# Slot work moved up behind the masks, three scatters a period, earlier fetches, and first-layer quarters in alternating PSUM tiles: a fused linear-attention and expert-layer kernel on one NeuronCore

## The chip, the cores and the metric

The kernel runs on one core of a Trainium2 chip. The metric is the device time of one execution in microseconds (us), lower is better; three runs of the kernel before took 453.21, 453.23 and 459.25 us, median 453.23. The engines are TensorE (PE; its weight loads are PEld), VectorE (DVE), ScalarE (ACT), GpSimd (POOL) and SyncE (SP), which here issues loads. ScalarE and GpSimd issue transfers too; those with row indices (gathers and scatters) come from GpSimd.

## The reference

The first half is causal linear attention with a decay for each head, over 4 batches, 8 heads, 768 tokens and head size 64, in blocks of 64. The second half gives each of the 3072 tokens (512 features) to one of 8 experts and applies that expert's two layers.

```python
# attention, for each block of 64 positions
intra = ((qb @ kb^T) * Dmask) @ vb                 # Dmask[i,j] = lam^(i-j) for i >= j
inter = (qb * lam^(pos+1)) @ kv_state
out[block] = intra + inter
kv_state = lam^64 * kv_state + (kb * lam^(63-pos))^T @ vb
# experts
logits = x @ w_gate + modality_bias[modality_id]
e_idx  = argmax(logits);  gate_w = softmax(logits)[e_idx]
for e in range(8):
    mask = e_idx == e
    out[mask] = gate_w[mask] * (relu(x[mask] @ w1[e]) @ w2[e])     # w1: 512x1024, w2: 1024x512
```

All in float32.

## The kernel before, in words

**Attention loop (0 to about 108 us).** The 24 chunks of 128 tokens (six a batch) are worked in 12 pairs, one a *period* (`for j in range(1, pairs + 1)`). A period issues the pair's `scores` (TensorE), `masked` (VectorE), `keys` and `queries` (VectorE), `from_state`, two `outputs` (TensorE, with a ScalarE copy each), `key_values` (TensorE), and `carried` (GpSimd multiplies the old state into `faded`, L265; VectorE adds). In between it turns the pair before into token rows: `tokens` (L296, TensorE, with a ScalarE copy to `xn`, L297), which also carry the gate's products, and go to the DRAM table `xs`. `gated` (VectorE) sums the gate's products of the pair before that.

**Slots.** After a batch's last pair, `route` finds each token's expert as a one-hot `oh` (VectorE); `ranks` counts on TensorE how many tokens stand before it; `places` (VectorE) makes of this the row `sloti` of the token in a table `inv` in DRAM (an area for each expert) and the gate's weight in `pay`, with one exponential on ScalarE, and adds the batch's counts to `ohsum`. `write_slot` scatters one chunk's 128 entries to `inv` by an indirect DMA (L390, on GpSimd), so 24 in all; before the change `places` comes after the state's products, `sloti` has one buffer, and there are two scatters a period. After two batches `early_list` counts tokens per expert (`count_tiles`) and names two full tiles of 256 tokens of one expert each: **A0** and **A1**. Their expert is in `listA`; A0's weights w1 and w2 (2 MB each, four loads into `raw1`, `raw2`) are fetched in the loop, `fetch_idx` (L567, SP) reads a tile's token numbers from `inv`, and `fetch_rows` (L577, GpSimd) gathers its token rows from `xs` into `xg`.

**Expert tiles.** A float32 matmul is made of three in fp32r (`three`, L617, L620, L621): high times high, high times low, low times high. `split` makes the two parts of an operand: a ScalarE cast (L549) and a VectorE subtraction (L550). A *wide* tile turns 256 rows (`turn_rows`, TensorE transposes L610 and two splits to `xh`, `xl`), does its first layer in four quarters, **q0** to **q3**, of 24 matmuls each (`wide`), whose results ScalarE takes as `hh` (L637, relu) and VectorE as the low part `hl` (L638), with the split of a quarter of w2 behind each (`tail`); then the second layer (`second`, 96 matmuls of 512 columns) from `hh`, `hl`, `w2h`, `w2l`. PSUM has two buffers of the name `s`; before the change q0 and q1 share the first, q2 and q3 the second.

**The order of the stages.** A0's first layer; the slots of the last two batches (`write_slots`, `places`, L366 to L383), a second count and `late_list`, a chain of small VectorE operations that makes the list of all other tiles, `listB`; A1's first layer; two *thin* tiles (64 and 32 rows) with weights from the list; then ten wide tiles, the first of which I call **tile 4**; then up to seven more that run only if needed. The list's last row is written at L537. Weights of a next tile are fetched (L594, L600, L721, on SP) when the tile's regs have been read.

**What sets the order.** A scheduler places the instructions of each engine; `pinned` ties an operation behind the one pinned before it on the same engine, and `behind(a, b)` a behind b (with `wait=False`: only its place, not a wait). In `wide` of the kernel before nothing is pinned.

Of the kernel before, what the change touches and what calls it, by code (L numbers as in the profile page):

```python
# [6 lines left out]
F32 = mybir.dt.float32  # L7
# [8 lines left out]
P = 128  # L16
# [3 lines left out]
HB = 2  # L20
# [20 lines left out]
def linear_attention_moe(tc, qkv, lam, modality, wg, mbias, w1, w2, out):  # L41
    nc = tc.nc
    with ExitStack() as ctx:
# [288 lines left out]
        def ranks(b, l, mxb, m8, oh, after=None):  # L332
# [11 lines left out]
            rk = ps.tile(shape, F32, name="kv" if after is None else "x", bufs=1)  # L344
            mm = pinned(nc.tensor.matmul(rk, lowb, oh, start=True, stop=False))
            if after is not None:
                behind(mm, after, wait=False)
# [5 lines left out]
        def places(b, l, mxb, m8, oh, rk):  # L353
# [12 lines left out]
            nc.vector.tensor_tensor(out=pos, in0=oh, in1=rk, op=ALU.mult)  # L366
            slot = t2("slot")
            nc.vector.tensor_reduce(out=slot, in_=pos, axis=AX, op=ALU.add)
            sloti = t2("sloti", I32)
# [3 lines left out]
            nc.vector.tensor_tensor(out=sloti, in0=slot, in1=m8s, op=ALU.add)  # L373

            pinned(nc.vector.tensor_tensor(out=l, in0=l, in1=mxb, op=ALU.subtract))
            nc.scalar.activation(out=l, in_=l, func=AF.Exp)
            sm = t2("sm")
            nc.vector.tensor_reduce(out=sm, in_=l, axis=AX, op=ALU.add)
            nc.vector.tensor_scalar(out=sm, in0=sm, scalar1=1e-9, scalar2=None, op0=ALU.add)
            nc.vector.reciprocal(out=pay[:, cs, 1].bitcast(F32), in_=sm)  # L380
            ohn = work.tile([P, E], F32, name="ohn", bufs=1)
            pinned(nc.vector.tensor_reduce(out=ohn, in_=oh.rearrange("p c e -> p e c"), axis=AX, op=ALU.add))
            nc.vector.tensor_tensor(out=ohsum, in0=ohsum, in1=ohn, op=ALU.add)  # L383
            return [(b * NC + c, sloti[:, c : c + 1]) for c in range(NC)]
# [13 lines left out]
        def count_tiles(first, nm):  # L398

            cp = ps.tile([P, E], F32, name="o", bufs=2) if nm == "A" else ps.tile([P, E], F32, name="kv", bufs=1)  # L400
# [39 lines left out]
        def early_list():  # L440
# [4 lines left out]
            nc.vector.tensor_scalar(out=delta, in0=full, scalar1=-1.0, scalar2=float(CAP // TT), op0=ALU.mult, op1=ALU.add)  # L445
            _, ex, at = tile_list(full, delta, None, EARLY, "A", ends)
            taken = const.tile([1, EARLY], F32, name="taken")
            nc.vector.tensor_copy(out=taken, in_=ex)
            nc.vector.tensor_scalar(out=ex, in0=ex, scalar1=float(E - 1), scalar2=None, op0=ALU.min)
            nc.vector.tensor_copy(out=listA[:, 0, :], in_=ex)  # L450
            nc.vector.tensor_scalar(out=listA[:, 1, :], in0=at, scalar1=float(TT), scalar2=None, op0=ALU.mult)
            nc.vector.tensor_tensor(out=listA[:, 2, 1:], in0=ex[:, 1:], in1=ex[:, : EARLY - 1], op=ALU.not_equal)
# [3 lines left out]
            nc.vector.tensor_tensor(out=took, in0=sidx[:, :E].unsqueeze(2).to_broadcast(sh),  # L456
                                    in1=taken.unsqueeze(1).to_broadcast(sh), op=ALU.is_equal)
            nA = const.tile([1, E], F32, name="nA")
            nc.vector.tensor_reduce(out=nA, in_=took, axis=AX, op=ALU.add)
            yield ex, nA  # L460

        def late_list(exA, nA):

            cnt, n2 = count_tiles(XT + 1, "B")
# [83 lines left out]
        def split(src, hi, lo, after=None, late=False):  # L548
            cp = nc.scalar.copy(out=hi, in_=src)  # L549
            df = nc.vector.tensor_tensor(out=lo, in0=src, in1=hi.bitcast(F32), op=ALU.subtract)  # L550
            if after is not None:
                behind(cp, after)
            if late:
                behind(cp, copies[-1], wait=False)
                behind(df, logits[-1], wait=False)
            return cp, df
# [35 lines left out]
        def fetch_w1(er, kw, after=None):  # L592
            for i in range(4):
                ld = nc.sync.dma_start(out=raw1[i], in_=w1[bass.ds(er, 1), :, i].rearrange("o p k f -> p (o k) f"), **kw)  # L594
                if after is not None:
                    behind(ld, after)
# [7 lines left out]
        def turn_rows(cols, before=None, part=range(2)):  # L604
            for i in part:
# [8 lines left out]
                split(tp[:, :, :cols], xh[i][:, :, :cols], xl[i][:, :, :cols])  # L614

        def three(out, ah, al, bh, bl, first, last, before=None):
            mm = nc.tensor.matmul(out, ah, bh, start=first, stop=False)  # L617
            if before is not None:
                behind(mm, before, wait=False)
            nc.tensor.matmul(out, ah, bl, start=False, stop=False)  # L620
            return nc.tensor.matmul(out, al, bh, start=False, stop=last)  # L621

        def wide(tail, before=None):

            for i in range(4):
                if i % 2 == 0:
                    pair = ps.tile([P, 2, 2, TT], F32, name="s", bufs=2)
                hp = pair[:, i % 2]
# [6 lines left out]
                if i == 0:  # L635
                    begun = mm
                act = nc.scalar.activation(out=hh[i], in_=hp, func=AF.Relu)  # L637
                nc.vector.scalar_tensor_tensor(out=hl[i], in0=hp, scalar=0.0, in1=hh[i].bitcast(F32),  # L638
                                               op0=ALU.max, op1=ALU.subtract)
                tail(i, act)  # L640
            return begun, mm
# [64 lines left out]
        def tail(i, act):  # L706
            for op, urgent in zip(split(raw2[i], w2h[i], w2l[i]), (act, ranked[-1])):
                behind(op, urgent, wait=False)
# [68 lines left out]
        routed, slots = None, []  # L777
# [59 lines left out]
        for j in range(1, pairs + 1):  # L837
            last = j == pairs
            turns = turned(j - 1)
            gs = (HB * j, HB * j + 1)  # L840
            if not last:
                sps = [scores(g) for g in gs]
# [208 lines left out]
```

## Time and profile before

| | |
|---|---|
| runs | 453.21, 453.23, 459.25 us; median 453.23 |
| profiled execution | 452.03 us, of which the span is 450.1 us |
| busy in the span | PE 409.3 us (91%), DVE 245.3 (55%), ACT 182.6 (41%), POOL 102.7 (23%) |
| attention loop | 0 to 108 us |
| A0 | first layer 122.24 to 143.87 us, second to 154.84 |
| A1 | first layer 154.84 to 171.11 us |
| thin tiles, then tile 4's first layer | from 171 us; tile 4's second layer begins at 213 |
| the other wide tiles | 213 to the end |

The span runs from the first to the last instruction; the rest of an execution's time lies around it. A row of a timeline gives start, duration, engine, line and operation with output and inputs, and in brackets how long the engine had been idle before it and what ended that. The clock (PEclk) is the share of full speed that was granted to TensorE: 1.00 is 2.4 GHz, about 0.5 is 1.2 GHz.

### The profile page before, as it was taken

The page shows a single profiled execution, that of the slowest core. Times are in us where ns is not written, and L with a number is a line of the kernel's source. Part 1 is how long each engine was busy: PE and PEld are TensorE (multiplying, and loading weights), DVE is VectorE, ACT ScalarE, POOL GpSimd, SP SyncE. Part 2 cuts the span into 40 slices and gives each one's busy share as a digit, 9 for nine tenths or more (in the row PEclk, how much of TensorE's full clock was granted, in tenths as well). Part 3 has the DMA queues.
Part 4 walks back from the last instruction along what each step waited for, and adds up shares of the span by engine and source line. Part 5 has one row for each costly group of instructions (what it writes and reads, how often), then busy time and mean ns, then how long its engine had stood idle before and what let it go on. Part 6 is the DMA issues. An engine that isn't in the chain of part 4 may idle for free. (4 is left out here: it accounts for less than half of the span.)

```text
span 450.1 us, 9891 instructions
## 1 busy us (share of the span) xinstructions
PE 409.3 (91%) x3864; PEld 362.3 (81%) x3864; DVE 245.3 (55%) x431; ACT 182.6 (41%) x277; POOL 102.7 (23%) x116
## 2 busy tenths in 40 slices
PE   8899999996677989997999999999999999999880
PEld 4699989895476878686898989898989989998760
DVE  4677877885188551166374655646372819090510
ACT  1124232244274131256363736455454637372410
POOL 5010134251366330050202020202011111101010
PEclk9999999999596999998999999999999999999995
DMA  6999998988400023711205466501111111101000
GB/s 206 352 367 386 374 365 300 369 285 302 123 29 2 26 84 128 294 34 26 74 23 167 164 225 247 212 27 51 48 50 48 51 47 43 48 1 48 1 28 17
DMA packets 25654, 63.84 MB, mean 142 GB/s; under 512 B 7157, under 2 KB 8701, under 8 KB 25600
## 3 DMA queue, kind: packets, MB, share of 16 engines
q1 hardware_dynamic: 17360, 43.36, 27.5%
q0 software_dynamic: 4768, 13.08, 9.0%
q10 hardware_dynamic: 3472, 6.69, 3.9%
q8 instruction: 32, 0.52, 0.5%
q14 instruction: 22, 0.18, 0.1%
HBM read 91.40 MB, written 14.07 MB: 234 GB/s over the span
## 5 line engine op out<-in xcount | busy, mean ns | idle before, releaser
L617 PE MATMUL s<-xh,w1h 128*128 128x256 f32 x384 | 112.2, 292 | 10.8 <-DVE hl L638 10.2
L621 PE MATMUL s<-xh,w1l 128*128 128x256 f32 x384 | 109.8, 287 | 1.2 <-DVE w1l L550 1.2
L620 PE MATMUL s<-xl,w1h 128*128 128x256 f32 x384 | 110.0, 287 | 0.0
L550 DVE TENSOR_TENSOR w1l<-raw,w1h 128x1024 fp32r<-128x1024 f32 x48 | 58.4, 1227 | 87.9 <-ACT w1h L549 87.2
L617 PEld LDWEIGHTS s<-xh,w1h 128*128 128x128 f32 x384 | 74.7, 195 | 16.6 <-DVE hl L638 15.5
L621 PEld LDWEIGHTS s<-xh,w1l 128*128 128x128 f32 x384 | 74.6, 194 | 1.6 <-DVE w1l L550 1.6
L617 PE MATMUL o<-w2h,hh 128*128 128x512 f32 x192 | 75.7, 394 | 0.0
L620 PEld LDWEIGHTS s<-xl,w1h 128*128 128x128 f32 x384 | 74.8, 195 | 0.6 <-issue 0.2
L621 PE MATMUL o<-w2h,hl 128*128 128x512 f32 x192 | 74.8, 389 | 0.0
L620 PE MATMUL o<-w2l,hh 128*128 128x512 f32 x192 | 74.7, 389 | 0.0
L549 ACT CAST w1h<-raw 128x1024 fp32r<-128x1024 f32 x48 | 49.8, 1051 | 36.4 <-PE s L620 23.3
L550 DVE TENSOR_TENSOR w2l<-raw,w2h 128x1024 fp32r<-128x1024 f32 x48 | 58.5, 1219 | 2.0 <-ACT w2h L549 2.0
L549 ACT CAST w2h<-raw 128x1024 fp32r<-128x1024 f32 x48 | 49.9, 1039 | 0.0
L638 DVE SCALAR_TENSOR_TENSOR hl<-s,hh 128x512 fp32r<-128x512 f32 x48 | 32.9, 685 | 25.4 <-ACT hh L637 25.4
L700 ACT ACTIVATE y<-o,idx 128x512 f32<-128x512 f32 x20 | 13.8, 690 | 79.0 <-PE o L621 46.2
L701 POOL DMA_INDIRECT out_dram<-y,idx x20 | 20.2, 1008 | 111.7 <-ACT y L700 107.3
L577 POOL DMA_INDIRECT xg<-xs,idx x20 | 21.8, 1092 | 91.2 <-PE kv L610 86.3
L621 PEld LDWEIGHTS o<-w2h,hl 128*128 128x128 f32 x192 | 36.0, 188 | 7.6
L620 PEld LDWEIGHTS o<-w2l,hh 128*128 128x128 f32 x192 | 36.1, 188 | 7.1
L617 PEld LDWEIGHTS o<-w2h,hh 128*128 128x128 f32 x192 | 36.1, 188 | 7.1
L390 POOL DMA_INDIRECT inv<-pay,sloti x24 | 31.7, 1321 | 34.4 <-PE o L285 8.2
L637 ACT ACTIVATE hh<-s 128x512 fp32r<-128x512 f32 x48 | 28.5, 594 | 26.9 <-PE s L621 26.9
(213 smaller groups left out, 470.1 us busy)
## 6 DMA issues: line engine op xcount, KB each, us to landing
raw<-in_w_dram SPq DMA_DIRECT2D x104, 512.0 KB
load<-in_qkv_dram SPq DMA_DIRECT2D x11, 2048.0 KB
xs<-xn ACTq DMA_DIRECT2D x24, 272.0 KB
load<-in_qkv_dram SPq DMA_DIRECT2D x4, 512.0 KB
w1h<-in_w_dram SPq DMA_DIRECT2D x4, 512.0 KB
w1l<-in_w_dram SPq DMA_DIRECT2D x4, 512.0 KB
dk<-tab_d SPq DMA_DIRECT2D x2, 256.0 KB
inv<-pad SPq DMA_DIRECT2D x2, 196.0 KB
```

Of the source, the lines that this page charges most:

```text
L390: sc = nc.gpsimd.indirect_dma_start(out=inv, out_offset=bass.IndirectOffsetOnAxis(ap=at, axis=0), in_=pay[:, c, :], in_offset=None)
L549: cp = nc.scalar.copy(out=hi, in_=src)
L550: df = nc.vector.tensor_tensor(out=lo, in0=src, in1=hi.bitcast(F32), op=ALU.subtract)
L577: last = nc.gpsimd.indirect_dma_start(out=(to or xg)[t][:m], out_offset=None, in_=xs[:rows, :], in_offset=bass.IndirectOffsetOnAxis(ap=idx ...
L617: mm = nc.tensor.matmul(out, ah, bh, start=first, stop=False)
L620: nc.tensor.matmul(out, ah, bl, start=False, stop=False)
L621: return nc.tensor.matmul(out, al, bh, start=False, stop=last)
L637: act = nc.scalar.activation(out=hh[i], in_=hp, func=AF.Relu)
L638: nc.vector.scalar_tensor_tensor(out=hl[i], in0=hp, scalar=0.0, in1=hh[i].bitcast(F32), op0=ALU.max, op1=ALU.subtract)
L700: nc.scalar.activation(out=y, in_=yp, func=AF.Copy, scale=idx[:, t, 1:2].bitcast(F32))
L701: sc = nc.gpsimd.indirect_dma_start(out=out, out_offset=bass.IndirectOffsetOnAxis(ap=idx[:, t, 0:1], axis=0), in_=y, in_offset=None, bound ...
```

## The change

- `places` becomes a generator with all its operations pinned. In the loop it comes right behind the masks, in the same period as `ranks`, and its second half (the exponential and what follows) behind the first token copy. `sloti` has two buffers.
- A third `write_slot` stands in the period, behind the second outputs.
- w1 of A0 is fetched without waiting for the last load of qkv; the index loads come before w2's load, which waits for A0's gather. The casts and low parts of w1's first two quarters stand within the last period. The loop ends one period sooner, and what remained of the last one is written out after it.
- The count for `early_list` uses an `s` tile in PSUM in place of `o`.
- `wide` takes two `s` tiles at once and gives q0 and q2 halves of the first, q1 and q3 halves of the second; `three` is pinned, and in A0 the evictions and the splits of w2 are too. The pins are cleared before the tiles that run only if needed.
- In A0, the old slots are written behind q0's matmuls, `ranks` and `places` of the last batch come behind q1's eviction, the second scatters and the count behind q2's. A1's token turns and its w1 splits are pinned ahead of `late_list`.

```diff
-        def ranks(b, l, mxb, m8, oh, after=None):
+        def ranks(b, l, mxb, m8, oh):
...
+            sloti = work.tile([P, NC], I32, name="sloti", bufs=2)
...
+            yield None
+            pinned(nc.scalar.activation(out=l, in_=l, func=AF.Exp))
...
+            yield [(b * NC + c, sloti[:, c : c + 1]) for c in range(NC)]
...
         def three(out, ah, al, bh, bl, first, last, before=None):
-            mm = nc.tensor.matmul(out, ah, bh, start=first, stop=False)
+            mm = pinned(nc.tensor.matmul(out, ah, bh, start=first, stop=False))
...
+        def wide(tail, before=None, pin=False):
+
+            two = [ps.tile([P, 2, 2, TT], F32, name="s", bufs=2) for _ in range(2)]
             for i in range(4):
-                if i % 2 == 0:
-                    pair = ps.tile([P, 2, 2, TT], F32, name="s", bufs=2)
-                hp = pair[:, i % 2]
+                hp = two[i % 2][:, i // 2]
...
+        def first_tail(i, act, mm, pin):
+
+            tail(i, act, mm, pin)
+            if i == 0:
+                begun.append(mm)
+                write_slots(slots, mm)
+            elif i == 1:
+                begun.append(places(*routed, ranks(*routed)))
+                next(begun[1])
+            elif i == 2:
+                write_slots(next(begun[1]), begun[0])
+                begun.append(count_tiles(XT + 1, "B"))
...
+            sps = [scores(g) for g in gs]
+            if routed is not None:
+                rk = ranks(*routed)
+            pts = [masked(g, sp) for g, sp in zip(gs, sps)]
+            if routed is not None:
+                placing, routed = places(*routed, rk), None
+                next(placing)
...
+            xts[gs[1]], mm = outputs(gs[1], pts[1], op)
+            write_slot(mm)
...
             if j == early + 1:
+                er, _ = fetch_regs(listA, 0, True)
                 fetch_w1(er, {}, loads[-1])
-                fetch_w2(er, {}, loads[-1])
             elif j == early + 2:
                 for i in range(EARLY):
                     fetch_idx(listA, i, idxA[i], after=loads[-1])
-                fetch_rows(idxA[0], TT, SOON * S, after=fades[-1])
...
+                fetch_w2(er, {}, fetch_rows(idxA[0], TT, SOON * S, after=fades[-1]))
...
+            turned = wide(first_tail if n == 0 else tail, before, n == 0)
             if n + 1 < fixed_ones:
                 ahead = range(EARLY, wides + 1) if n == 0 else range(n + 2, min(n + 3, fixed_ones))
                 if n == 0:
+                    turn_rows(TT, turned, pin=True)
+                    for i in range(4):
+                        split(raw1[i], w1h[i], w1l[i], True)
+                    late_list(*begun[2], exA, nA)
```

TensorE in A1's first layer: where one quarter ends and another begins. `s_2258` is the first of the two PSUM tiles, `w1h` and `w1l` with their number are a quarter's parts of w1. Before:

```order
L621 MATMUL s_2258<-xh1_147,w1l0_134 128x256
L617 MATMUL s_2315<-xh0_146,w1h2_132 128x256
...
L617 MATMUL s_2315<-xh0_146,w1h2_132 128x256
L617 MATMUL s_2258<-xh0_146,w1h1_131 128x256
...
L621 MATMUL s_2258<-xh1_147,w1l1_135 128x256
L620 MATMUL s_2315<-xl0_148,w1h2_132 128x256
```

and now:

```order
L619 MATMUL s_2258<-xh1_147,w1l0_134 128x256
L615 MATMUL s_2259<-xh0_146,w1h1_131 128x256
...
L619 MATMUL s_2259<-xh1_147,w1l1_135 128x256
L615 MATMUL s_2258<-xh0_146,w1h2_132 128x256
...
L619 MATMUL s_2258<-xh1_147,w1l2_136 128x256
L615 MATMUL s_2259<-xh0_146,w1h3_133 128x256
```

Before, q2 was begun behind q0 and finished behind q1; now the quarters follow in the order of their numbers, each in the other tile than the one before it.

VectorE in A0's first layer, where the evictions, the splits of w2 and the last batch's slot work stand together. `x_1952` and `x_1896` are the ranks, `cntB` is the second count. Before:

```order
L638 SCALAR_TENSOR_TENSOR hl0_1830<-s_1832,hh0_1828 128x512
...
L366 TENSOR_TENSOR pos_1960<-oh_1792,x_1952 128x48
L638 SCALAR_TENSOR_TENSOR hl0_1830<-s_1832,hh0_1828 128x512
L368 TENSOR_REDUCE slot_1962<-pos_1960 128x6
L383 TENSOR_TENSOR ohsum_120<-ohsum_120,ohn_1974 128x8
L550 TENSOR_TENSOR w1l1_135<-raw11_123,w1h1_131 128x1024
L550 TENSOR_TENSOR w2l_1827<-raw21_127,w2h_1826 128x1024
L638 SCALAR_TENSOR_TENSOR hl1_1831<-s_1889,hh1_1829 128x512
...
L403 COPY cntB_1985<-kv_1983 1x8
```

and now:

```order
L633 SCALAR_TENSOR_TENSOR hl0_1830<-s_1833,hh0_1828 128x512
L548 TENSOR_TENSOR w2l_1827<-raw21_127,w2h_1826 128x1024
L364 TENSOR_TENSOR pos_1904<-oh_1796,x_1896 128x48
...
L375 TENSOR_TENSOR ohsum_120<-ohsum_120,ohn_1913 128x8
L633 SCALAR_TENSOR_TENSOR hl1_1831<-s_1832,hh1_1829 128x512
L548 TENSOR_TENSOR w2l_1827<-raw22_128,w2h_1826 128x1024
...
L402 COPY cntB_1957<-kv_1955 1x8
```

The slot work now stands in one piece between q1's and q2's evictions, and the splits of w1 for A1 have gone from between them.

GpSimd at the end of the loop: the scatters of batch 1, the state's multiplications and A0's gathers. Before:

```order
L390 DMA inv_114<-pay_107,sloti_1235 24832x8 x2
L265 TENSOR_TENSOR faded_1457<-state2_118,pq_102 128x256
L390 DMA inv_114<-pay_107,sloti_1235 24832x8
L265 TENSOR_TENSOR faded_1590<-state0_116,pq_102 128x256
L390 DMA inv_114<-pay_107,sloti_1235 24832x8
L265 TENSOR_TENSOR faded_1593<-state1_117,pq_102 128x256
L390 DMA inv_114<-pay_107,sloti_1235 24832x8
L577 DMA xg0_138<-xs_113,idxA0_152 128x544
```

and now:

```order
L388 DMA inv_114<-pay_107,sloti_1214 24832x8 x3
L265 TENSOR_TENSOR faded_1450<-state2_118,pq_102 128x256
L388 DMA inv_114<-pay_107,sloti_1214 24832x8
L265 TENSOR_TENSOR faded_1587<-state0_116,pq_102 128x256
L265 TENSOR_TENSOR faded_1590<-state1_117,pq_102 128x256
L573 DMA xg0_138<-xs_113,idxA0_152 128x544
```

The last scatter of the batch now stands ahead of the last period's two multiplications.

## Rows read from the trace of the kernel before

**Rows 1.** The profile's first line, and the granted clock in 40 equal slices of the span, in tenths of full speed.

```profile
span 450.1 us, 9891 instructions
...
PEclk9999999999596999998999999999999999999995
```

**Rows 2.** The view of stretches: window in us, its length, busy us (and instructions) of PE, PEld, DVE, ACT and POOL, granted clock, share of the DMA engines, GB/s.

```profile
108.00:122.24 14.24, 5.54 (x33) 3.93 (x31) 4.09 (x6) 4.23 (x8) 4.03 (x4) 0.64 0.40 121
122.24:143.87 21.63, 15.98 (x123) 15.19 (x121) 16.82 (x55) 10.81 (x15) 12.61 (x10) 0.84 0.11 36
143.87:154.84 10.97, 10.97 (x52) 9.09 (x50) 7.52 (x32) 3.48 (x6) 4.58 (x4) 1.00 0.08 27
154.84:171.11 16.27, 14.12 (x105) 13.60 (x104) 6.34 (x10) 5.19 (x7) 4.99 (x5) 0.90 0.21 58
...
213.00:423.00 210.00, 207.45 (x1339) 188.41 (x1337) 111.84 (x122) 107.09 (x141) 34.94 (x34) 1.00 0.26 84
```

**Rows 3.** The timeline of TensorE: start, duration, operation, and in brackets the idle time before it and what ended it; rows that had waited.

```profile
59.18 0.68 PE L296 MATMUL x<-iw,xt 128*64 128x136 f32 x8 [0.69 <-ACT xn L297]
...
83.33 0.68 PE L296 MATMUL x<-iw,xt 128*64 128x136 f32 x8 [0.69 <-ACT xn L297]
...
115.66 0.45 PE L610 MATMUL x<-ident,xg 128*128 128x128 f32 x1 [7.43 <-DMA xg<-xs,idxA]
116.90 0.90 PE L610 MATMUL x<-ident,xg 128*128 128x128 f32 x3 [0.80 <-DMA xg<-xs,idxA]
...
135.20 0.17 PE L401 MATMUL kv<-ohsum,onesb 128*128 128x8 bf16 x1 [2.13 <-DVE ohsum L383]
...
138.07 0.58 PE L617 MATMUL s<-xh,w1h 128*128 128x256 f32 x1 [2.71 <-DVE hl L638]
...
160.09 0.39 PE L617 MATMUL s<-xh,w1h 128*128 128x256 f32 x1 [0.72 <-DVE hl L638]
...
166.69 0.58 PE L617 MATMUL s<-xh,w1h 128*128 128x256 f32 x1 [1.43 <-DVE hl L638]
...
208.05 0.58 PE L617 MATMUL s<-xh,w1h 128*128 128x256 f32 x1 [3.13 <-DVE hl L638]
...
423.29 0.39 PE L617 MATMUL s<-xh,w1h 128*128 128x256 f32 x1 [2.18 <-DVE hl L638]
```

**Rows 4.** The timelines of GpSimd and SP from the last scatters of batch 1 to A0's gathers, and of ScalarE and VectorE at the second half of A0's token rows.

```profile
94.44 1.01 POOL L390 DMA_INDIRECT inv<-pay,sloti  x1 [0.16 <-issue]
...
101.73 1.01 POOL L390 DMA_INDIRECT inv<-pay,sloti  x1 [0.16 <-DMA raw<-in_w_dram]
...
108.21 0.98 SPq L567 DMA_DIRECT2D idxA<-inv  x2
...
112.05 1.04 POOL L577 DMA_INDIRECT xg<-xs,idxA  x1 [9.32 <-issue]
113.40 1.00 POOL L577 DMA_INDIRECT xg<-xs,idxA  x1 [0.31 <-issue]
...
118.69 0.59 ACT L549 CAST xh<-kv 128x512 fp32r<-128x512 f32 x1 [0.27 <-PE kv L610]
...
119.31 0.69 DVE L550 TENSOR_TENSOR xl<-kv,xh 128x512 fp32r<-128x512 f32 x1 [0.16 <-ACT xh L549]
```

**Rows 5.** The timeline of TensorE again: the first and the last of the 96 first-layer matmuls of a wide tile at full clock, and two of A0's at the low clock, 19 matmuls apart.

```profile
224.05 0.28 PE L617 MATMUL s<-xh,w1h 128*128 128x256 f32 x1
...
235.63 0.28 PE L621 MATMUL s<-xh,w1l 128*128 128x256 f32 x1
...
138.45 0.42 PE L620 MATMUL s<-xl,w1h 128*128 128x256 f32 x1
...
142.51 0.37 PE L621 MATMUL s<-xh,w1l 128*128 128x256 f32 x1
```

**Rows 6.** The timeline of VectorE in A0, and the last row of the list.

```profile
128.89 0.68 DVE L638 SCALAR_TENSOR_TENSOR hl<-s,hh 128x512 fp32r<-128x512 f32 x1
129.49 1.22 DVE L550 TENSOR_TENSOR w2l<-raw,w2h 128x1024 fp32r<-128x1024 f32 x1
...
134.13 0.20 DVE L366 TENSOR_TENSOR pos<-oh,x 128x48 f32<-128x48 bf16 x1
...
134.99 0.16 DVE L383 TENSOR_TENSOR ohsum<-ohsum,ohn 128x8 bf16<-128x8 bf16 x1
...
152.38 0.16 DVE L537 TENSOR_SCALAR listB<-ats 1x21 int32<-1x21 f32 x1
```

**Rows 7.** The timeline of SP: the issues of the loads of w1 behind the list, and of the thin tile's own weights.

```profile
167.01 1.23 SPq L594 DMA_DIRECT2D raw<-in_w_dram  x4
...
174.45 2.13 SPq L721 DMA_DIRECT2D w1h<-in_w_dram  x4
```

**Rows 8.** The view of stretches while those weights come in; columns as in rows 2.

```profile
176.00:178.00 2.00, 2.00 (x11) 1.65 (x10) 0.00 (x0) 0.69 (x1) 0.23 (x1) 1.00 0.91 297
...
180.00:182.00 2.00, 2.00 (x10) 1.46 (x8) 0.00 (x0) 0.00 (x0) 0.00 (x0) 1.00 0.90 322
```

**Rows 9.** The timeline of VectorE in tile 4's first layer.

```profile
206.17 1.23 DVE L550 TENSOR_TENSOR w2l<-raw,w2h 128x1024 fp32r<-128x1024 f32 x1 [0.24 <-ACT w2h L549]
207.31 0.69 DVE L638 SCALAR_TENSOR_TENSOR hl<-s,hh 128x512 fp32r<-128x512 f32 x1
```

**Rows 10.** The scatters of the slots as one group by line: durations in ns (least, median, longest), then the first and the last start in us.

```profile
L390 POOL DMA_INDIRECT inv<-pay,sloti x24: 954/1112/2447, 60.0 to 146.6; - x24
```

More of the change, by code (lines that the diff above doesn't have):

```diff
@@ L341, in t2 @@
                 return work.tile([P, NC], dt, name=nm, bufs=1)
[L344 to L347, printed above, removed]
+            rk = ps.tile(shape, F32, name="x" if b == B - 1 else "kv", bufs=1)
+            pinned(nc.tensor.matmul(rk, lowb, oh, start=True, stop=False))
             pinned(nc.tensor.matmul(rk, onesb, ohsum.unsqueeze(1).to_broadcast(shape), start=False, stop=False))
@@ L365, in places @@
             pos = t3("pos")
[L366 to L369, printed above, removed]
+            pinned(nc.vector.tensor_tensor(out=pos, in0=oh, in1=rk, op=ALU.mult))
             m8s = t2("m8s")
@@ L545, in late_list, with split @@
             nc.vector.tensor_copy(out=nums, in_=many)
-        def split(src, hi, lo, after=None, late=False):
+        def split(src, hi, lo, pin=False):
             cp = nc.scalar.copy(out=hi, in_=src)
             df = nc.vector.tensor_tensor(out=lo, in0=src, in1=hi.bitcast(F32), op=ALU.subtract)
[L551 to L555, printed above, removed]
+            if pin:
+                pinned(cp)
+                pinned(df)
             return cp, df
@@ L595, in fetch_w1 @@
                 if after is not None:
-                    behind(ld, after)
+                    behind(ld, after, wait=after not in loads)
         def fetch_w2(er, kw, after=None):
@@ L880, in linear_attention_moe @@
                 next(listing)
+            xts[gs[1]], mm = outputs(gs[1], pts[1], op)
+            write_slot(mm)
+            next(turns)
+            kp, _ = key_values((gs[1], gs[1] + 1))
+            mm = next(turns)
+            for g in (gs[1], gs[1] + 1):
+                carried(g, kp)
+            write_slot(mm)
             more(LOADS + j)
@@ L935, in run @@
             idx = idxs.get(n) or get_idx(n)
-            begun, turned = wide(tail, before)
-            if n == 0:
-                write_slots(slots, begun)
-                write_slots(places(*routed, ranks(*routed, begun)))
-                late_list(exA, nA)
+            turned = wide(first_tail if n == 0 else tail, before, n == 0)
             if n + 1 < fixed_ones:
@@ L961, in run_early @@
             idx = idxA[n]
-            _, whole = wide(tail)
+            whole = wide(tail)
             fetch_w2(*regs(EARLY))
```

141 lines of the change are left out of this document (67 added, 74 removed).

## The prediction

> **What bounds the kernel now.** The page's first two parts come first [rows 1]: TensorE is busy nearly throughout, and the granted clock dips to 0.5 or 0.6 of full speed (1.2 instead of 2.4 GHz) in two of the slices between 110 and 135 us of the 450.1 us span. Then the view of stretches [rows 2]: from 213 us on TensorE is busy 207.45 of 210 us at clock 1.00, so that part has nothing to give. The stretches from 108 to 213 us hold idle time and low clock. Then TensorE's own timeline, reduced to the rows that had to wait [rows 3]: 7.43 us for the gathered token rows, then waits for VectorE's low parts (`hl`) and for the counts of the slots, and in the token loop two of 0.69 us for a token copy. I call the two early tiles A0 and A1, the first wide tile after the two thin ones tile 4, and a quarter of the first layer q0 to q3.
>
> **Attention loop.** Both 0.69 us waits [rows 3] fall in periods where ScalarE held a token copy behind the exponential, which waited for VectorE. The change puts the slot work right behind the masks and the exponential behind the copy; with two `sloti` buffers VectorE no longer waits for old scatters either. Sum: 2 x 0.69 = **-1.4 us**. VectorE now does the slot work before keys and queries; those are wanted only when `key_values` comes, so I cost that at nothing. If the cover is short, TensorE waits there at most 1 us in each of three periods.
>
> **Up to A0's first matmul.** Today the last scatter of batch 1 ends at 101.73 + 1.01 = 102.74 us; the index load goes at 108.21, the two gathers at 112.05 and 113.40 [rows 4], and the second's rows are used at 116.90 [rows 3]: 14.2 us from end to use. With three a period that scatter is the third of its period, behind a `faded` on GpSimd, where the row at 94.44 [rows 4] stands now: end 95.45 - 1.4 = 94.1 us, 8.7 us earlier. If each transfer takes as long as today, the rows come at 108.2. w2's 2 MB are no longer in flight then (its load waits for this gather), so they may come earlier: at about 104 if scatter, index load and gather each land in the 2.5 us that lie between the second gather's end (114.40) and 116.90. TensorE is done with the loop's outputs at 108.2 - 1.4 = 106.8, has 1.0 us of token turns to do first, and so waits 0 to 0.4 us where it waited 8.2. Eight transposes (0.8), then the second half's cast (0.59) and low part (0.69) [rows 4]: q0 starts near 110.5 instead of 122.24. That is 11.7 us, of which 1.4 is counted above; I take **-10 us**. Bounds: -8 if the transfers take 2 us more in other company, -10.5 if nothing is late.
> The Trainium skill (DMA: Bandwidth & Descriptors, Queues, rings and completion order) says that each DMA engine takes turns between its queues packet by packet, so that a small transfer need not stand behind a bulk load; by that, taking w2 away would speed nothing and the sum would be the 108.2 one. The row speaks otherwise: 5.5 us from the scatter's end to the index load.
>
> **A0's first layer.** From 122.24 to 143.87 is 21.63 us [rows 2]. A matmul follows the other every 0.122 us at full clock (95 steps from 224.05 to 235.63), every 0.214 us at the low clock (19 steps from 138.45 to 142.51) [rows 5]; four quarters of 24 are 11.7 us, eight transposes 0.8, ranks and count 0.4: 12.9. What VectorE is late with now: the ranks wait for the one-hot, behind which q0's `hl` stands in line, about 1.0 us (an estimate from seven routing operations of 0.20 us with their gaps); the count waits for `ohsum`, which follows a low part (0.68), a w2 split (1.22) and seven operations of 0.16 to 0.20 us [rows 6]: 1.4 us. So 15.3 against 21.6: **-6.3 us**. Bounds: -8.7 without those waits, -3.9 with them doubled. The casts of w2 stand in ScalarE's fixed order, and hold it if w2 is late: the load goes at 108.2, and 2 MB took about 7.5 us from the issue at 174.45 [rows 7, 8], a quarter each 1.6 us; w2's first piece is there at about 111, wanted at 114. Covered by 3 us.
>
> **A1.** 154.84 to 171.11, 16.27 us [rows 2]; work 11.7 + 0.4. TensorE runs q0, q2, q1, q3 there, ScalarE and VectorE evict q0, q1, q2, q3, hence the 0.72 and 1.43 us waits [rows 3] and the low clock behind them. After the change all three agree and the next quarter in a tile comes a whole quarter (2.9 us) after the eviction it needs: **-4.2 us** (-2.1 if half of it stays). The new list must be ready in time. VectorE then does, from the count at 122.1 on (110.5 + 8.8 + 0.4 + 2.4), two `hl`, two w2 splits, some seventeen small operations (together 6.4), two `xl` (1.2), with 0.5 of waiting, then A1's four w1 splits (4.9) and the rest of the list (about 6, an estimate from some forty operations of 0.16 us): 141.1, where the list's last row ended at 152.54 [rows 6]. A1's q0 starts at 125.8 + 10.97 = 136.8, so the list is 6 to 7 us later relative to A1 than today, and A1 only just does not wait for what hangs on it.
>
> **Thin tiles.** What follows the list keeps its distances [rows 7]: from 152.54 it takes 14.5 us to the w1 issue at 167.01, then, with nothing queued ahead, about 3 us to the loads of the thin tile's own weights, and 7.5 us until the first 2 MB are in (about 300 GB/s [rows 8]). That is 166.1. TensorE wants them at 136.8 + 11.7 + 11.0 + 3.6 + 0.6 = 163.7 (A1's two layers, the first thin product, a token turn that now stands before the second): 2.4 us late, of which the moved turn gives 0.6 back: **+1.8 us** (0 to +4).
>
> **Tile 4 and the last tile.** The same mismatch of orders made VectorE finish a quarter's `hl` only after another's w2 split [rows 9], and TensorE wait 3.13 us at 208.05; sixteen matmuls then ran at the low clock, 16 x 0.092 = 1.5. Both go: **-4.6 us**. The last tile's 2.18 us wait [rows 3]: **-2.2 us**. In the tiles between, all engines agreed already: 0.
> I add **+1.5 us** for one stretch at the low clock somewhere in 108 to 125 us, since new waits of 1 us stand there close together.
>
> **Sum.** -1.4 - 10 - 6.3 - 4.2 + 1.8 - 4.6 - 2.2 + 1.5 = -25.4 us. The profiled execution took 452.03 us, giving 426.6; the median of the runs, 453.23, is 1.2 above it: **428 us**. All good ends (-10.5, -8.7, 0 for the thin tiles and for the clock) give 422 on the same footing. All bad ones together (3 us more in the loop, -8, -3.9, -2.1, +4, +3 for the clock) give 441.
>
> **Rivals.**
> 1. *The gather stays late.* The index load waits for all twelve scatters; if the last one is held on GpSimd or lands late, TensorE idles some 7 us again at the low clock. For it: today's 5.5 us. Against: 8.7 us of lead. 428 + 8 = 436. Chance 0.10.
> 2. *The scatters of batches 2 and 3 stretch.* Twelve now run in a row from 113.4 on, beside a VectorE that never rests. Their durations go from 0.95 to 2.45 us, median 1.11 [rows 10], plus 0.3 between two. At the median they end at 131 and land before the list; at the longest, 113.4 + 12 x 2.75 = 146.4, plus 2.3 to land, and the index loads go 7 us late; with a low-clock stretch 428 + 8.5 = 436.5. Chance 0.08. The Trainium skill (SBUF — State Buffer, SBUF: two separate sides) says that a VectorE operation with two SBUF inputs and a GpSimd instruction hold their shared port in turn, the loser blocked throughout; that speaks against this change, and the spread of the row agrees in kind.
> 3. *Both 1 and 2*: 428 + 16.5 = 444.5, within 2%. Chance 0.08.
> 4. *Slower.* Every wide tile now writes q2 into the bank pair that q0's eviction has just left. If the eviction comes later than one quarter, as it does today where ScalarE casts the next w1 first, each of the ten later wide tiles gets tile 4's stall: 3.13 + 1.5 us, 46 us in all, 474. It decides once the eviction ends more than 2.9 us after its quarter. Against it: today's order has the same distance and 213 to 423 us shows 2.55 us idle in all [rows 2]. Chance 0.04.
> 5. *The reorder does nothing on the chip* because a later engine re-creates the wait: in rivals 1 and 3.
>
> **Chances.** Forecast 0.70, rivals as above. Faster by over 2% (under 444.2; 2% is about what a measurement of this kernel can tell): 0.70 + 0.10 + 0.08 = 0.88; within 2%: 0.08; slower: 0.04. Range 420 to 438: from a little under all good ends to almost all bad ones; it takes in rivals 1 and 2 and leaves out 3 and 4 (0.12) and the tails.
>
> **What would show it.** TensorE's wait for `xg` under 1.5 us and its q0 of A0 near 110; no 3 us wait for `hl` anywhere; q0 to q3 evicted in order; the list's last row near 140; TensorE's first wait for thin weights around 164; the low-clock stretches down from four in 108 to 213 us to one or two. A wait for `xg` over 5 us, an index load that waits for scatters after 141, or `hl` waits in every wide tile would make the prediction wrong.

## The result: 429.3 us, forecast 428

The changed kernel takes 429.28 us (median of four runs, 429.02 to 434.81) against 455.26 of the kernel before on the same occasions: a ratio of 0.945, 95% interval 0.934 to 0.956, faster by over 2%. The profiled execution took 429.08 us, its span is 427.4 us. The page of the changed kernel, first line and granted clock, against [rows 1]:

```profile
span 427.4 us, 9911 instructions
...
PEclk9899999999999999999999999999999999999995
```

The two dips are gone. The view of stretches of the changed kernel, cut where its own stages begin (columns as in rows 2):

```profile
108.00:116.94 8.94, 4.47 (x54) 3.17 (x51) 2.43 (x4) 3.94 (x10) 2.00 (x2) 1.00 0.82 276
116.94:130.65 13.71, 12.96 (x114) 12.71 (x113) 11.57 (x34) 7.61 (x12) 8.49 (x7) 1.00 0.31 118
130.65:141.66 11.01, 11.01 (x51) 9.10 (x50) 10.94 (x42) 6.40 (x9) 9.48 (x6) 1.00 0.02 3
141.66:153.50 11.84, 11.84 (x102) 11.63 (x100) 8.13 (x22) 5.58 (x8) 5.88 (x6) 1.00 0.18 55
153.50:180.11 26.61, 25.20 (x229) 17.93 (x227) 5.45 (x9) 6.61 (x11) 4.61 (x5) 1.00 0.57 203
180.11:192.99 12.88, 12.51 (x107) 12.31 (x105) 10.61 (x11) 8.79 (x13) 5.86 (x3) 1.00 0.18 46
192.99:402.00 209.01, 208.37 (x1351) 189.64 (x1350) 114.53 (x125) 108.61 (x143) 36.62 (x34) 1.00 0.26 85
```

The stages are: up to A0's q0, A0's first and second layer, A1's first layer, A1's second layer with the thin tiles, tile 4's first layer, the rest. Only the first still has TensorE idle for half its length.

One thing has to be taken out before stages are compared. TensorE's second scores need only the first loads, and start at a different time in each execution: from 21.1 to 25.2 us in the profiles of this study, whatever the kernel. In the two profiles, before and then changed:

```profile
21.61 2.06 PE L232 MATMUL s<-load 64*128 64x128 f32 x32
```

```profile
23.14 2.06 PE L232 MATMUL s<-load 64*128 64x128 f32 x32
```

The changed kernel's profile began 1.53 us later. Below, "from the start" means from there. The last outputs of the loop begin at 106.03 us before and at 106.40 now. So the spans differ like this:

| stage | before | changed | difference | forecast |
|---|---|---|---|---|
| first loads, up to the second scores | 21.61 | 23.14 | +1.5 | 0 |
| attention loop, to its last outputs | 84.42 | 83.26 | -1.2 | -1.4 |
| from there to q0 of A0 | 16.21 | 10.54 | -5.7 | -10 |
| A0's first layer | 21.63 | 13.71 | -7.9 | -6.3 |
| A1's first layer | 16.27 | 11.84 | -4.4 | -4.2 |
| A1's second layer and thin tiles | 24.34 | 26.61 | +2.3 | +1.8 |
| tile 4's first layer | 17.62 | 12.88 | -4.7 | -4.6 |
| from there to the end, last tile included | 237.03 | 234.41 | -2.6 | -2.2 |
| low clock in one new place | | | 0 | +1.5 |

With A0's second layer (10.97 and 11.01) these make -22.7 us, the difference of the spans; the forecast was -25.4. One term is far off, the third.

TensorE's timeline of the changed kernel, rows that waited:

```profile
111.12 0.68 PE L296 MATMUL s<-iw,xt 128*64 128x136 f32 x8 [1.27 <-ACT xn L297]
...
116.33 0.68 PE L296 MATMUL s<-iw,xt 128*64 128x136 f32 x8 [2.89 <-ACT xn L297]
...
126.91 0.17 PE L400 MATMUL kv<-ohsum,onesb 128*128 128x8 bf16 x1 [0.73 <-DVE ohsum L375]
...
170.34 1.91 PE L650 MATMUL s<-w1h,xf 128*32 128x256 f32 x26 [0.55 <-DMA w1h<-in_w_dram]
```

Of [rows 3] the long wait for `xg`, all waits for `hl` and the two in the loop are gone. In their place stand two waits for token copies (L297) ahead of q0. ScalarE and SP there:

```profile
109.95 2.47 SPq L596 DMA_DIRECT2D raw<-in_w_dram  x4
...
111.73 0.66 PE L606 MATMUL x<-ident,xg 128*128 128x128 f32 x4
...
114.54 0.33 ACTq L299 DMA_DIRECT2D xs<-xn  x1
114.91 0.59 ACT L547 CAST xh<-x 128x512 fp32r<-128x512 f32 x1 [2.67 <-DMA raw<-in_w_dram]
```

The first transposes of A0's rows start at 111.73 and end at 112.39, the cast that needs them starts at 114.91: ScalarE had waited 2.67 us, for w2's load. The cast does not read w2. Ahead of it on ScalarE stands the store of the token rows (L299), and in the built program that store waits for a completion counter (DMAHW6) which w2's first load, issued at 109.95, was the last to take:

```
L596 DMA raw_126<-in_w_dram 128x1024 [waits DMAHW6_49,DMASW5_49]
L299 DMA xs<-xn 128x544 [waits DMAHW6_49,Activation_49]
L547 CAST xh_146<-x 128x512 [waits PE_49]
```

### The profile page after: what moved, and what is told of

It is laid out like the page before. It is cut to its first block, busy times and chain, and to the rows that moved or that the text cites. A ratio compares the mean times of both kernels' runs of the same rounds, so it can differ in the third digit from the quotient of the medians.

```text
span 427.4 us, 9911 instructions
## 1 busy us (share of the span) xinstructions
PE 402.7 (94%) x3864; PEld 356.8 (84%) x3864; DVE 246.1 (58%) x431; ACT 182.6 (43%) x277; POOL 107.4 (25%) x116
## 4 chain that ended last, share of the span: by engine, by line
issue 48%; PE 20%; DMA 12%; POOL 8%; DVE 6%; SPq 2%; ACT 1%; POOLq 0%; ACTq 0%; DVEq 0%
PE s L232 5%; PE x L296 5%; PE o L285 5%; POOL out_dram L699 4%; DMA idx<-inv 4%; POOL xg L573 3%; DMA xg<-xs,idx 3%; PE o L278 3%; PE kv L252 2%; SPq L590 1%; DMA xg<-xs,idxA 1%; DMA raw<-in_w_dram 1%; DVE w1l L548 1%; DMA dk<-tab_d 1%; DVE w2l L548 1%
## 5 line engine op out<-in xcount | busy, mean ns | idle before, releaser
L615 PE MATMUL s<-xh,w1h 128*128 128x256 f32 x384 | 109.4, 285 | 0.7
L619 PE MATMUL s<-xh,w1l 128*128 128x256 f32 x384 | 107.9, 281 | 0.4 <-DVE w1l L548 0.4
L618 PE MATMUL s<-xl,w1h 128*128 128x256 f32 x384 | 107.8, 281 | 0.0
L548 DVE TENSOR_TENSOR w1l<-raw,w1h 128x1024 fp32r<-128x1024 f32 x46 | 55.6, 1225 | 84.4 <-ACT w1h L547 84.4
L615 PEld LDWEIGHTS s<-xh,w1h 128*128 128x128 f32 x384 | 72.3, 188 | 4.0 <-DVE hl L633 2.3
L619 PEld LDWEIGHTS s<-xh,w1l 128*128 128x128 f32 x384 | 72.4, 188 | 0.6 <-DVE w1l L548 0.6
L618 PEld LDWEIGHTS s<-xl,w1h 128*128 128x128 f32 x384 | 72.4, 188 | 0.4
L547 ACT CAST w1h<-raw 128x1024 fp32r<-128x1024 f32 x46 | 47.5, 1053 | 27.3 <-PE s L618 21.3
L573 POOL DMA_INDIRECT xg<-xs,idx x20 | 25.0, 1251 | 86.0 <-PE kv L606 74.8
L388 POOL DMA_INDIRECT inv<-pay,sloti x24 | 32.5, 1356 | 25.2 <-PE x L296 6.3
```

What stands on the lines that cost most here:

```text
L388: sc = nc.gpsimd.indirect_dma_start(out=inv, out_offset=bass.IndirectOffsetOnAxis(ap=at, axis=0), in_=pay[:, c, :], in_offset=None)
L573: last = nc.gpsimd.indirect_dma_start(out=(to or xg)[t][:m], out_offset=None, in_=xs[:rows, :], in_offset=bass.IndirectOffsetOnAxis(ap=idx ...
L615: mm = pinned(nc.tensor.matmul(out, ah, bh, start=first, stop=False))
L618: pinned(nc.tensor.matmul(out, ah, bl, start=False, stop=False))
L619: return pinned(nc.tensor.matmul(out, al, bh, start=False, stop=last))
```

## Experiments

**Is it the counter?** The store and the load get other counters; the instructions of every engine and their order stay:

```diff
-                fetch_w2(er, {}, fetch_rows(idxA[0], TT, SOON * S, after=fades[-1]))
+                first_rows = fetch_rows(idxA[0], TT, SOON * S, after=fades[-1])
...
+        fetch_w2(er, {}, first_rows)
         fetch_w1(*fetch_regs(listA, 1, False))
...
                     behind(ld, after)
+                    behind(ld, stores[-1], wait=False)
```

> The kernel as changed, but w2's load takes its completion counter behind the last stores of the token rows; the instructions of every engine and their order stay. Theory: ScalarE's store of the token rows waited for the counter that w2's first piece held, 2.67 us, and everything up to A0's first quarter stood behind it. Then the cast of A0's token rows comes within 0.3 us of its transposes (2.5 before), TensorE's wait of 2.89 us falls below 1, and the time goes from 429.1 to about 426.6. Rival: the store or the cast waits for the traffic of w2 itself, or for the chain of ScalarE's copies: the cast stays 2 us behind, and the time stays within 0.7 of 429.1.

Measured: 424.56 us (423.53 to 425.43), 0.929 of before (0.923 to 0.936). TensorE's and ScalarE's rows:

```profile
108.26 0.68 PE L296 MATMUL s<-iw,xt 128*64 128x136 f32 x8 [0.94 <-ACT xn L297]
...
109.41 0.33 ACTq L299 DMA_DIRECT2D xs<-xn  x1
109.92 0.59 ACT L547 CAST xh<-x 128x512 fp32r<-128x512 f32 x1 [0.54 <-PE x L607]
...
111.42 0.68 PE L296 MATMUL s<-iw,xt 128*64 128x136 f32 x8 [0.48 <-ACT xn L297]
112.03 0.39 PE L616 MATMUL s<-xh,w1h 128*128 128x256 f32 x1
```

The cast now waits for its transposes (from 108.88), the wait of 2.89 is 0.48. In the change w2's first piece lands at 114.47 us, by its counter in the trace, and the store goes at 114.54. From the start (22.00 here) q0 comes at 90.0 us instead of 93.8, 3.8 sooner, and the stages behind it keep their lengths. Two further profiles with the counter as in the change have q0 at 93.7 (e3 below, the same program up to there) and 94.1 (e10, the change again). The counter is shown as the cause, and its price is 3.8 us.

**What is left ahead of q0.** First A0's transposes ahead of the token turns, on top of the edit above:

```diff
+        turn_rows(TT, pin=True)
         next(turns)
         next(turns)
         gated(pairs - 2)
-        turn_rows(TT, pin=True)
```

> As e1_other_counter, and A0's token rows are transposed ahead of the last pair's four token turns. Theory (what is left up to A0's first quarter is ScalarE's chain of copies, five of 0.39 us, ahead of the cast): the transposes then wait for the gather alone, whose rows land near 109.9 us, q0 starts near 113 and the time is 2 us under e1, about 424.5. Rival (the routing behind the token turns is the longer chain): the ranks and the count then wait longer on VectorE in A0 by what q0 gains, and the time is e1's within 0.7 us.

Measured: 427.31 us (424.56 to 428.71). From the start (23.70) q0 comes at 115.58 - 23.70 = 91.9 us, 1.9 later than in e1: the transposes wait 0.87 us for the gather, and all four token turns with two waits for ScalarE's copies then stand between them and q0. My theory (424.5) fell, and the time is not the rival's either (within 0.7 of e1). That the order of the change is the better one shows in q0 of the two profiles only: the ratios to before, 0.927 to 0.941 here and 0.923 to 0.936 in e1, overlap.

**Order or tiles?** The quarters in order, but q0 and q1 in one PSUM tile:

```diff
-                hp = two[i % 2][:, i // 2]
+                hp = two[i // 2][:, i % 2]
```

> The kernel as changed, but q0 and q1 lie in one PSUM tile and q2 and q3 in the other; the pinned order q0 to q3 stays. Theory A (a matmul into one half of a tile is made to wait for the eviction of the other half, so the order alone would stall and the alternation is what makes it possible): q1 and q3 each wait for an eviction of some 1.3 us and its latency, in all twelve wide tiles, 24 x 1.5 = 36 us, and with low clock behind some of them more: 465 us or above. Theory B (the order is all that matters, the tiles are not): 429.1 within 0.7.

Measured: 514.76 us, 1.127 of before. The clock, the first-layer group (busy, mean ns, idle time before and its releaser) and two rows of TensorE:

```profile
PEclk9999999997999998998989889798897988979996
...
L615 PE MATMUL s<-xh,w1h 128*128 128x256 f32 x384 | 122.9, 320 | 57.5 <-DVE hl L633 57.5
```

```profile
221.71 0.39 PE L615 MATMUL s<-xh,w1h 128*128 128x256 f32 x1 [2.92 <-DVE hl L633]
...
230.58 0.58 PE L615 MATMUL s<-xh,w1h 128*128 128x256 f32 x1 [2.92 <-DVE hl L633]
```

A matmul into one half of a tile waits here until the other half's last reader is done: 57.5 us in twelve tiles. Behind the second wait of a tile thirteen matmuls take 0.41 us each instead of 0.28, at a granted clock of 0.50 (230.58 to 233.50 us; 1.00 in 221.71 to 227.50), so low clock comes on top. Theory A holds, at more than twice its price. That the order before (q0, q2, q1, q3) was the scheduler's way around this wait would fit, but no run shows it. The order without the alternating tiles does harm; the tiles without the order were not run.

**The first layer alone.** The kernel before with the alternating tiles and the pinned order of `wide` and `three` as in the diff above, nothing else.

> The kernel before, with the alternation and the pinned order of the first layer alone. Theory: A1 gives 4.4, tile 4 4.7 and the last tile 2.5 us, A0's first layer less than half of its 7.9 since VectorE's mixed order stays there, nothing before 122 us: 453.2 - 11.6 - 3 = 438.6, and the thin tiles give back 2 to 4 because A1 is done sooner and their weights are not: 441 to 443. Rival: the thin tiles' weights take all of A1's gain and tile 4's was due to the low clock alone: 447 or above.

Measured: 437.62 us (437.27 to 439.49), 0.958 (0.951 to 0.964). The view of stretches of this run:

```profile
110.00:126.58 16.58, 6.96 (x47) 4.90 (x41) 4.09 (x6) 4.85 (x9) 4.04 (x4) 0.66 0.41 126
126.58:140.80 14.22, 13.36 (x110) 13.21 (x109) 12.78 (x26) 11.40 (x16) 8.22 (x6) 0.91 0.07 22
...
152.27:164.11 11.84, 11.84 (x101) 11.63 (x99) 6.58 (x11) 5.57 (x8) 6.19 (x6) 1.00 0.23 72
164.11:190.20 26.09, 25.23 (x228) 17.88 (x227) 5.40 (x9) 6.60 (x11) 3.57 (x4) 1.00 0.55 199
190.20:203.14 12.94, 12.52 (x108) 12.32 (x105) 10.66 (x11) 8.85 (x13) 5.86 (x3) 1.00 0.18 45
```

A1, tile 4 and the thin tiles are what they are in the change. The time is some 3.4 us under what I expected (441 to 443). A0's first layer is 14.2 us instead of 21.6, 7.4 less, where I had expected less than half of the gain. Not all of it is shown to be the order of the quarters. With TensorE's order pinned, the ranks of the last batch (139.13) and the count (140.49) also went behind q3; before, they stood ahead of it, and the count waited 2.13 us [rows 3]. And A0's second layer grew from 10.97 to 11.47, so the two layers together gave 6.9. From the start the two profiles differ by 14.4 us (439.49 - 23.52 against 452.03 - 21.61): 16.8 gained behind q0 of A0, 2.4 lost ahead of it.

**The rest alone.** The change without the alternation: pairs, and `three` unpinned.

> The kernel as changed, with the first layer's quarters in pairs and unpinned as before: all of the change but the alternation. Theory (the two halves of the change add up): e4_wide_alone took 14.5 us off when the later start of its loads in the profiled execution is taken out, so this one is 14.5 over the change, 429.3 + 14.5 = 443.8, with the waits for low parts of about 1, 1.4, 3 and 2 us back in A0, A1, tile 4 and the last tile. Rival (the earlier slots and rows are worth nothing without the order, A0 waits for its evictions whenever it starts): 450 or above.

Measured: 447.61 us (440.2, 447.2, 448.0 and 449.0), between theory and rival. With one run at 440 and three at 447 to 449 no verdict follows, and whether the two halves add up stays open. The profile, of the run of 448.0, has waits for `hl` back in A1 (1.19 us) and tile 4 (3.13), and in A0 a longer wait for the count than before the change:

```profile
129.90 0.17 PE L400 MATMUL kv<-ohsum,onesb 128*128 128x8 bf16 x1 [3.92 <-DVE ohsum L375]
```

**Scatters and w2.** On top of e1, the third scatter of a period is taken out:

```diff
             xts[gs[1]], mm = outputs(gs[1], pts[1], op)
-            write_slot(mm)
```

> As e1_other_counter, with two scatters a period as before. Theory (what set A0's start was the last scatter of batch 1): it moves one period of 7.4 us later, the index load from 99.5 to about 107, q0 from 112.0 to 118 or 119, and the time is 424.6 + 6.5 = 431. Rival (with w2 no longer in flight the gather has slack): within 1.5 of 424.6.

And in the change itself w2's load is put back behind w1's:

```diff
                 fetch_w1(er, {}, loads[-1])
+                fetch_w2(er, {}, loads[-1])
...
-                fetch_w2(er, {}, fetch_rows(idxA[0], TT, SOON * S, after=fades[-1]))
+                fetch_rows(idxA[0], TT, SOON * S, after=fades[-1])
```

> The kernel as changed, with w2's load right behind w1's again, two periods sooner. Theory (small transfers land later beside a bulk load): the index load goes near 101 as it does with w1 alone in flight, but the gather's rows come 3 us later than in e1_other_counter, whose store does not wait either: 424.6 + 3 = 427.6. Rival (the landing does not depend on what else is in flight): q0 starts where e1's does and the time is 424.6 within 0.8.

Measured: 431.41 us (430.27 to 436.43) and 431.43 us (431.18 to 434.26). From the start q0 comes at 97.8 and 96.1 us, 7.8 and 6.1 later than in e1, so each of the two moves is needed. Against the kernel before (100.6) q0 is 2.8 us sooner with all but the third scatter, 4.5 with all but w2's move, 10.6 with both (e1). e5 met its theory (431); e6 came 3.8 us above its own (427.6). The timelines of GpSimd, SP and TensorE, with two scatters:

```profile
106.66 1.01 POOL L388 DMA_INDIRECT inv<-pay,sloti  x1 [0.16 <-issue]
...
108.81 1.23 SPq L563 DMA_DIRECT2D idxA<-inv  x2
```

and with w2 early:

```profile
93.18 1.01 POOL L388 DMA_INDIRECT inv<-pay,sloti  x1 [0.17 <-issue]
...
99.80 1.59 SPq L563 DMA_DIRECT2D idxA<-inv  x2
...
108.66 1.07 POOL L573 DMA_INDIRECT xg<-xs,idxA  x1 [8.41 <-DMA xs<-xn]
...
112.78 0.45 PE L606 MATMUL x<-ident,xg 128*128 128x128 f32 x1 [4.14 <-DMA xg<-xs,idxA]
```

The index load follows the scatter's end by 1.1 us where the weights were issued 13 us before it (95.85), and by 5.6 us where 4 MB had just been issued (89.60 and 92.62). With w1 alone in flight it was 5.0 in the change (scatter's end 95.93, index load 100.90). The scatter is what the index load waited for in the trace. So the scatter already lands this late with w1 alone in flight.

What differs with w2 is the next step: the gather is released 8.9 us after the index load's issue, 4.1 in the change. The row names a store of token rows, but in the built program the gather does not wait for that store. It waits for its index load, and the counters in the trace show when that landed: at 107.81 us, 8.0 after its issue, against 3.2 in the change (104.07) and 3.0 before (111.24). The gather follows the landing by 0.9 us in each of the three. In e6 the index load landed 0.2 us behind w2's last piece (107.60), which had been issued ahead of it on the same queue. So the time lies in the index load's landing behind w2; a shared counter, as in e1, has no part in it.

**The list and the token turns.** On top of e1, `late_list` ahead of A1's pinned splits (e7), and in addition two PSUM tiles for the last pair's four token turns, which share one otherwise (e8; e11 has that without e7's edit):

```diff
-                    turn_rows(TT, turned, pin=True)
-                    for i in range(4):
-                        split(raw1[i], w1h[i], w1l[i], True)
                     late_list(*begun[2], exA, nA)
+                    turn_rows(TT, turned, pin=True)
+                    for i in range(4):
+                        split(raw1[i], w1h[i], w1l[i], True)
...
+            if j == pairs - 1:
+                xp = [ps.tile([P, HB, 2, 256], F32, name="s", bufs=2) for _ in range(2)]
...
-                    yield tokens(HB * j + blk, hf, xts[HB * j + blk], xns[j], xp[:, hf] if j == pairs - 1 else at)
+                    yield tokens(HB * j + blk, hf, xts[HB * j + blk], xns[j], xp[hf][:, blk] if j == pairs - 1 else at)
```

> As e1_other_counter, with the late list ahead of A1's token splits and w1 splits on VectorE. Theory (the scatter of 5.43 us is held by the four w1 splits that run beside it, and the thin weights wait for the list): no scatter beside the list's small operations is over 2.5 us, the list's last row comes 4 us sooner, A1 does not wait since its first split is done before its q0, and the stretch from A1's second layer to tile 4 (26.3 us) falls by 1 to 1.5: 423.3. Rival: A1's q0 or q1 waits for its w1 splits as much as the thin tiles gain, and the time is 424.6 or above; or a scatter takes over 4 us all the same.

> As e7_list_first, and the last pair's four token turns alternate between two PSUM tiles. Theory (the waits of 0.94 and 0.48 us for a token copy are the same kind of wait as in e3_pairs_in_order, a half held by the other half's eviction): both go, q0 starts 0.7 to 1.4 us sooner than in e7, and the time is about 1 under e7's. Rival (the gathered rows are what comes last): the time is e7's within 0.4.

> As e1_other_counter, with the last pair's token turns alternating between two PSUM tiles and the list where the change has it. Theory (the alternation of the token turns is what made e8 faster, the list's place is worth nothing): 2.5 us under e1, 422, and q0 87.6 us behind the second scores' start. Rival (the two go together): e1's 424.6 within 0.8.

> The kernel as changed, unaltered, beside e11 on the same chip: 429 to 431, with q0 of A0 93.8 us behind the second scores' start.

> e8_both, unaltered, once more: whether its gain over e1_other_counter and e11_two_tiles stands on another occasion. Theory (list first and two tiles together are worth 2 us or more): 421.3 to 424.5, a ratio to the kernel before under 0.932. Rival (what e8 showed was a good execution): 425 to 427, as e1 and e11.

Measured: e7 425.46 us (423.55 to 426.94), e8 422.54 (421.34 to 426.01), e11 426.73 (425.55 to 428.16), the change again 429.51 (427.2 to 434.42), e8 again 423.30 (422.07 to 426.63). Against before: e8 0.927 (0.920 to 0.934) and 0.929 (0.925 to 0.934), e11 0.937 (0.933 to 0.941), the change 0.943 (0.938 to 0.948). So e8 is the fastest kernel here and beats both kernels, the one before and the changed one, on two occasions. The time of e7 missed its theory (423.3); e8 is 2.9 us under e7, where the theory said about 1; e8 again met its own, and the change again came back to its time. That e8 beats e1 (0.929) is not shown: the intervals overlap. e7 gave no gain in the thin tiles (26.36 us against 26.34): the list's last row ended only 1.0 us sooner after q0, since its last rows were placed among the splits, so the edit did not do what it was to do.

In e8 the 0.94 and 0.48 us waits are gone and q0 comes at 87.6 us from the start, 2.5 sooner than in e1; in e11, the same program up to there, it came at 91.2, behind a gather whose second issue took 2.06 us instead of 1.00 and a wait of 1.41 us for its rows. In e11 that issue began beside two subtractions of VectorE:

```profile
107.72 2.35 DVE L880 TENSOR_TENSOR w1l<-raw,w1h 128x1024 fp32r<-128x1024 f32 x2
...
107.76 2.06 POOL L573 DMA_INDIRECT xg<-xs,idxA  x1 [0.31 <-issue]
```

In e8 the same subtractions began at 104.70, behind the start of the gather's second issue (103.73). The time of e11 fits neither its theory (422) nor its rival (424.6). The gain of the two tiles thus hangs on when the gather goes and its rows land, and is not settled.

## Why the forecast held, step by step

- **Attention loop, -1.4:** -1.2. Both waits of [rows 3] are gone. Right.
- **Up to q0, -10:** the step that failed is the sum's "waits 0 to 0.4 us where it waited 8.2". The gather came as early as forecast (second issue at 106.35 us; 94.1 + 5.5 + 5.2 = 104.8 by the distances of [rows 4], and the later start is the 1.5 between), but the edit that moved w2 had a second effect that I had not thought of: I asked what w2 delays by its bytes, not who waits for its counter. -5.7 measured; e1 shows 3.8 of the missing 4.3 there. The cover of 3 us for w2's first cast, all that the prediction says for that edit, held and was beside the point.
- **w2's bytes:** I took the 5.5 us from scatter to index load in [rows 4] as w2's doing. In the change, with w2 gone, it is still 5.0. w2's part lies in the landing of the index load behind it (e6): 8.0 us against 3.2. The Trainium skill (DMA: Bandwidth & Descriptors, Queues, rings and completion order) says that each DMA engine takes turns between its queues packet by packet. The trace agrees in part: in the change the scatter, on GpSimd's queue, landed at 100.88 us, ahead of w1's last piece (103.25), but 5.0 us after its end, against 1.1 us with the weights issued long before (e5).
- **A0, -6.3:** -7.9. The waits of 1.0 and 1.4 us that I put in came to 0.73 in all. I put the loss down to the slot work; e4, which does not move that work on VectorE, has 7.4 of the 7.9. But it also takes the ranks and the count, with their wait of 2.13 us, out from among the quarters on TensorE, so how much is the order of the quarters and how much the slot work stays open.
- **Low clock, +1.5:** none from 108 to 402 us in the changed kernel's view of stretches; waits of 1.27 and 2.89 us stood close together and the clock stayed at 1.00. This (1.5 us) and A0 (1.6) made good 3.1 of the 4.3 us that q0 lost. That 428 came out nearer than its terms was luck.
- **A1, tile 4, last tile, -4.2, -4.6, -2.2:** -4.4, -4.7, -2.6. Right, and e4 has A1 and tile 4 as short as the change. The reason that I gave, that the orders agree, is only part of it: in e3 they agree, two quarters share a tile, and the waits come in every tile. For tile 4 I had counted sixteen matmuls at the low clock; the trace before has thirteen (208.05 to 210.77), about 1.2 us instead of 1.5.
- **Thin tiles, +1.8:** +2.3. The list's last row ended 27.2 us after q0 (144.0 + 0.17 - 116.94; forecast 30.6), the w1 issue followed at 158.23, 14.1 later (14.5), the thin weights' loads at 161.57, 3.3 later (3). But TensorE lost only about 1.2 us at the thin weights themselves, half of the forecast 2.4: that product takes 3.02 us from its first to its last matmul, 1.87 before. The other 1.1 stand in the two token turns ahead of it. So the size is right partly for another reason.
- **Rivals:** none came. Rival 2 came in small: one scatter of twelve stretched (below), before the list was done, at no cost that shows: the last scatter ended at 142.06, the list's last row at 144.17, and the index loads went at 145.46. Rival 4 has its counterpart in e3: 85 us, had the change kept the pairs.
- **Where the low clock was:** the second of the two dips in [rows 1] is the slice from 135.0 to 146.3 us, not between 110 and 135 as I read it. Nothing in the sum hangs on it.

## To carry to other kernels

When a transfer is moved, list not only whose bytes it competes with but which completion counter it takes and who issues next on that counter: a store on a busy engine can stand behind a load it has nothing to do with, and everything on that engine behind the store. Where evictions and matmuls share PSUM tiles, fix order and tiles together, and run each without the other; here only the order was run alone. And take out what differs from one execution to the next before stages are compared, here the first loads.

## What the runs showed of the hardware

A GpSimd instruction that begins with a run of VectorE subtractions can last as long as the run. VectorE and GpSimd in the changed kernel:

```profile
134.08 4.61 DVE L548 TENSOR_TENSOR w1l<-raw,w1h 128x1024 fp32r<-128x1024 f32 x4
...
134.09 5.44 POOL L388 DMA_INDIRECT inv<-pay,sloti  x1 [0.30 <-issue]
```

and in e7, where the scatters are through by then and a store of results is next:

```profile
135.21 5.84 POOL L700 DMA_INDIRECT out_dram<-y,idxA  x1 [0.30 <-issue]
135.22 1.21 DVE L548 TENSOR_TENSOR w1l<-raw,w1h 128x1024 fp32r<-128x1024 f32 x1
...
138.96 1.21 DVE L548 TENSOR_TENSOR w1l<-raw,w1h 128x1024 fp32r<-128x1024 f32 x1
```

In ten of the profiles an issue that begins with the run of four takes 5.43 to 5.84 us. It is not so each time: in e3 two scatters begin within the same run and take 2.02 and 1.97 us.

```profile
137.59 4.61 DVE L548 TENSOR_TENSOR w1l<-raw,w1h 128x1024 fp32r<-128x1024 f32 x4
...
137.61 2.02 POOL L388 DMA_INDIRECT inv<-pay,sloti  x1 [0.30 <-issue]
139.93 1.97 POOL L388 DMA_INDIRECT inv<-pay,sloti  x1 [0.31 <-issue]
```

The other issues in these profiles take 0.95 to 2.2 us. In the kernel before, the splits had gaps between them and the longest scatter took 2.45 us [rows 10]. The Trainium skill (SBUF — State Buffer, SBUF: two separate sides) says that a VectorE operation with two SBUF inputs and a GpSimd instruction that reads SBUF lock a shared port, each for its whole instruction. The trace agrees in kind. In the changed kernel GpSimd did not get its turn between four subtractions of 1.2 us that follow each other without a gap, and lost 4.4 us at once; in e3 it did. What decides is open.
